# Linear attention with RMS norm and a Gelu feed-forward layer: two batches' keys without padding rows, Gelu's table loaded one step earlier

## The chip, the cores and the metric

The kernel runs on one core of one Trainium2 chip. The metric is the time of one execution on the device in microseconds (us). TensorE (PE in the profile) multiplies matrices, VectorE (DVE) and ScalarE (ACT) work element by element, GpSimd (POOL) helps them, and SyncE (SP) issues the transfers between the main memory and the core's own memory, which 16 DMA engines carry out.

## The reference

For each of 8 batches and 8 heads, keys and values of 576 rows are multiplied to a 64x64 matrix, the queries are multiplied by it, and the result is normed along the head. The heads side by side give 4608 rows of 512 numbers, which pass through a feed-forward layer with 2048 inner units and an exact Gelu. All is float32.

```python
# q, k, v: (8, 8, 576, 64); w_in: (512, 2048); w_out: (2048, 512)
kv = np.einsum('bhsd,bhse->bhde', k, v)
out = np.einsum('bhsd,bhde->bhse', q, kv)
rms = np.sqrt(np.mean(out * out, axis=-1, keepdims=True) + 1e-06)
x = (out / rms * g_norm).transpose(0, 2, 1, 3).reshape(8 * 576, 512)
h = x @ w_in
g = 0.5 * h * (1.0 + erf(h / np.sqrt(2)))
y = g @ w_out
```

## The kernel before

**Tiles and stages.** The 4608 rows are cut into seven chunks: two of 512 (`PLAIN`) and five of 704 or 736. A chunk's attention output is made while the chunk before goes through the feed-forward layer, so that TensorE always has matmuls. For the first chunk there is no chunk before: its keys, queries and weights have to arrive first, and this start-up is where the change lies.

**Keys and values.** They are summed over a batch's 576 rows in `sum_kv` (line 198), for one pair of heads at a time. The rows are split as 4 x 112 + 128. The 4 x 112 come as one tile, `kv_main[b, p]`, of 112 used partitions (`KROWS`) by 1024 numbers, which the host has padded with zeros to 128 partitions; the last 128 rows come as `kv_tail`. `load_kv(b, p)` issues both (line 161 for the main tile, lines 166 and 178 for the tail). Whatever the tile holds, TensorE reads its first 112 partitions only: line 162 cuts the view to `[:KROWS]`.

**The order of the transfers** is the order in which SyncE's instructions are written: batch 0's four key tiles with the first chunk's queries among them, the first weight, batch 1's first two pairs, the second weight (`w_in`), the first `w_out` and the next `w_in`, batch 1's other two pairs, then the remaining weights in turn. `load_w` (line 617) loads a weight. At most eight transfers are in flight: SyncE waits for the landing of the eighth before.

**The order of the work** on each engine is the order of the code; nothing is reordered. For the first chunk: `sum_first(p)` sums a pair's keys and `place_kv` copies the result (lines 209 on ScalarE, 211 on VectorE); `project_first` multiplies the queries (line 252). Then come the squares, their sums, and the reciprocal root (line 315 and three operations of VectorE). The first two blocks of the output are scaled on VectorE (lines 361, 864). For the other two, ScalarE spreads the roots (line 852), TensorE transposes them (line 872) and VectorE multiplies (line 874). Ahead of the transposes TensorE sums batch 1's first two pairs (line 198).

**The weights** arrive as 64-bit floats. `top_w(n)` (line 631) is a pass of ScalarE over a weight's upper halves, with Prelu; `bits_w(n)` (lines 641, 644) is VectorE's part, and gives the number in 32 bits. From that `high_w` (line 652, ScalarE) and `low_w` (line 656, VectorE) make a high and a low part. The output of the attention is split in the same way: `high_x` (line 369) makes four casts on ScalarE, `low_x` (line 374) four differences on VectorE.

**The feed-forward layer** of the first chunk: `layer1` multiplies by a block of the first weight (line 666 for the first two blocks, line 676 for the others), `gelu` applies Gelu twice on ScalarE (lines 689, 690), `rest` takes the low part on VectorE (line 696), `layer2` multiplies by the second weight (line 708). [...] The dummy Gelu at line 857, on two numbers, makes the compiler put the load of Gelu's table there (`ACT_TABLE_LOAD`) and not ahead of the first real Gelu.

Of the kernel before, what the change touches and what calls it, by code (L numbers as in the profile page):

```python
# [11 lines left out]
AF = mybir.ActivationFunctionType  # L12
# [4 lines left out]
P = 128  # L17
EPS = 1e-6
CH = 512
KROWS = 112  # L20
# [19 lines left out]
def linear_attn_rms_gelu_ffn(  # L40
# [18 lines left out]
    nc = tc.nc  # L59
# [66 lines left out]
    def block_tile(name, dtype):  # L126
        if name not in home:
            raise KeyError(name)
        width = 2 * WIDEST if name[0] == "d" else 2 * DM
        return home[name].tile([P, width], dtype, name=name)  # L130
# [3 lines left out]
    def late_tile(name):  # L134

        if name not in late:
            late[name] = block_tile(name, I32).bitcast(F32)
        return late[name]
# [11 lines left out]
    def load_kv(b, p):  # L150

        early = b == 0 or (b == 1 and p > 1)
        if early:
            main = late_tile(f"w_out{NF - 1 - p if b == 0 else NF - 3 - p}")
        elif b == PLAIN and p > 1:
            main = block_tile(f"x{2 + p}", F32)
        elif b == PLAIN + 1 and p > 1:
            main = block_tile(("w_in7", "w_out4")[p - 2], F32)
        else:
            main = low.tile([P, 2 * DM], I32, name="kv_main", bufs=2).bitcast(F32)  # L160
        nc.sync.dma_start(out=main, in_=kv_main[b, p])
        main = main.rearrange("p (a n) -> p a n", a=2)[:KROWS]
        if b == 0:
            tails = late_tile(f"w_in{NF - 1}")[:TAIL].rearrange("p (a n) -> p a n", a=NP)
            if p == 0:
                nc.sync.dma_start(out=tails, in_=kv_tail[0])
            tail = tails[:, p]
        else:
            if early:
                tail = late_tile(f"w_in{NF - 5}")[:, (p - 2) * 2 * P:(p - 1) * 2 * P]  # L170
            elif b >= PLAIN and p > 1:
                if p == 2:
                    kv_ps["tails"] = block_tile(SPARE[2], F32)
                tail = kv_ps["tails"][:, (p - 2) * 2 * P:(p - 1) * 2 * P]
            else:
                tail = low.tile([P, 2 * P], I32, name="kv_tail", bufs=2).bitcast(F32)
            tail = tail[:TAIL]
            nc.sync.dma_start(out=tail, in_=kv_tail[b, :, p])
        tail = tail.rearrange("p (a n) -> p a n", a=2)
        parts = [main[:, :, j * P:(j + 1) * P] for j in range(NJ)] + [tail]  # L180
        kv_in[b, p] = [(t[:, 0], t[:, 1]) for t in parts]
# [440 lines left out]
    def top_w(n):  # L622


        zs[n] = work.tile([P, WIDEST], I32, name="z", bufs=2)[:, :DM]
        top = raw[n].rearrange("p (n two) -> p n two", two=2)[:, :, 1]
        if n < FULL:
            z = late_tile(f"w_out{NF - 1}")[:, n * DM:(n + 1) * DM]
        else:
            z = work.tile([P, WIDEST], F32, name="w", bufs=2)[:, :DM]  # L630
        nc.scalar.activation(  # L631
            out=zs[n].bitcast(F32), in_=top.bitcast(F32), func=AF.Prelu,
            scale=2.0 ** -112, alpha=2.0 ** 32,
        )
        ws[n] = z.bitcast(I32)
# [91 lines left out]
    g_row = late_tile(f"w_in{NF - 6}")[:1, P:2 * P]  # L727
    ones, eps = (late_tile(f"w_in{NF - 6}")[:1, a * P:(a + 1) * P] for a in (2, 3))
    load_kv(0, 0)
    first.load(0)  # L730
    load_kv(0, 1)
    first.load(1)
    for p in (2, 3):
        load_kv(0, p)
# [32 lines left out]
    for d in range(0, 2 * D, BLK):  # L767
        h = d // D * D
        nc.gpsimd.tensor_tensor(
            out=fold[:, d:d + BLK], in0=ident[:, h:h + BLK], in1=ident[:, h + BLK:h + 2 * BLK],  # L770
# [24 lines left out]
    def column(n, t):  # L795
        return n_fold + 2 * ((n - 2) * NG + t)

    def sum_squares(n):
# [12 lines left out]
        out=half_g, in0=ps[:, :1], scalar1=0.5, scalar2=None, op0=ALU.mult  # L811
# [3 lines left out]
        out=sums[:, :P], lhsT=ones, rhs=eps, start=True, stop=False,  # L815
# [4 lines left out]
        out=root_g, in0=half_g, scalar1=D ** 0.5, scalar2=None, op0=ALU.mult  # L820
# [9 lines left out]
    for half in range(2):  # L830
# [6 lines left out]
        out=sums[:, :n_fold].rearrange("p (g b) -> p g b", g=2), lhsT=fold,  # L837
# [3 lines left out]
    for half in range(2):  # L841
        nc.scalar.activation(
            out=first.block((1, half)),
            in_=first.ps.pop((1, half)).rearrange("p (a n) -> p a n", a=2), func=AF.Copy,
# [4 lines left out]
    for n in (2, 3):  # L849
        roots[n] = low.tile([P, CH], F32, name="gh", bufs=2)  # L850
        at = column(n, 0)
        nc.scalar.copy(
            out=roots[n].rearrange("p (c d) -> p c d", d=D),
            in_=first.inv[:, at:at + 2 * NG].unsqueeze(2).broadcast_to((P, 2 * NG, D)),
        )
    top_w(1)
    nc.scalar.activation(out=eps[:, :2], in_=ones[:, :2], func=AF.Gelu)

    kv_ps[1, 0] = next_bank("a")
    sum_kv(1, (0, 1), kv_ps[1, 0])  # L860
    for half in range(2):
# [3 lines left out]
            out=first.o_all[:, half], in0=first.ps.pop((0, half)), scalar=root_g, in1=bc,  # L865
# [656 lines left out]
```

## Time and profile before

| what | value |
|---|---|
| median of 3 runs | 742.12 us (740.96 to 743.08) |
| the profiled execution | 741.02 us |
| its span, first to last instruction | 739.2 us |
| TensorE busy | 732.6 us (99%) |
| VectorE, ScalarE, GpSimd busy | 528.1, 357.3, 122.6 us |
| chain that ended last | TensorE 93%, transfers 3% |
| transfers | 233.66 MB, 316 GB/s on average |

The profile's page divides the span into 40 slices of 18.5 us. The chain that ended last is found by going back from the last instruction, at each step to whatever released it. An idle stretch is named with what ended it, in brackets behind an instruction. Of the 1.8 us between the profiled execution's time and its span the trace shows nothing.

### The profile page before, as it was taken

How to read it: one execution, taken by the hardware profiler on the slowest of the kernel's cores; microseconds unless marked ns; L12 is line 12 of the kernel's file. 1: busy time of each engine (PE TensorE's matmuls, PEld its weight loads, DVE VectorE, ACT ScalarE, POOL GpSimd, SP SyncE). 2: the span in 40 equal slices, each digit the busy share in tenths (PEclk: the TensorE clock that was granted, in tenths of full speed). 3: DMA queues.
4: the chain of work that ended last, by engine and by line, in shares of the span. 5: the costliest groups of instructions: out<-in, count | busy, mean ns of one | idle time of the engine just before them, and what ended most of it. 6: DMA issues, size and time to landing. Idle time of an engine off the chain costs nothing.

```text
span 739.2 us, 13288 instructions
## 1 busy us (share of the span) xinstructions
PE 732.6 (99%) x5150; PEld 696.3 (94%) x5150; DVE 528.1 (71%) x756; ACT 357.3 (48%) x565; POOL 122.6 (17%) x88
## 2 busy tenths in 40 slices
PE   8999999999999999999999999999999999999998
PEld 6888888888899999999999999999999999999997
DVE  3999998999857689357599257598257598254773
ACT  3788845643465367054365154365154364133640
POOL 1000000000045800013800014600015600022000
PEclk9999999999999999999999999999999999999999
DMA  9998985689998999988999978999978889988893
GB/s 343 407 408 284 364 283 200 220 313 359 346 335 314 361 336 387 408 317 282 323 325 371 406 243 271 313 326 361 395 230 281 276 291 310 335 295 289 295 318 121
DMA packets 84962, 233.66 MB, mean 316 GB/s; under 512 B 8484, under 2 KB 29476, under 8 KB 84900
## 3 DMA queue, kind: packets, MB, share of 16 engines
q1 hardware_dynamic: 84896, 232.82, 88.6%
q8 instruction: 41, 0.67, 0.4%
q14 instruction: 21, 0.17, 0.1%
q10 hardware_dynamic: 4, 0.00, 0.0%
HBM read 193.99 MB, written 38.80 MB: 315 GB/s over the span
## 4 chain that ended last, share of the span: by engine, by line
PE 93%; DMA 3%; DVE 1%; ACT 1%; issue 1%; ACTq 0%; DVEq 0%
PE banks_Z L1276 15%; PE banks_Z L1184 14%; PE acc L708 11%; PE h L676 10%; PE banks_X L1184 10%; PE banks_Y L1184 10%; PE banks_X L1276 10%; PE banks_Y L1276 9%; DMA w_out<-kv_main 1%; DMA w_in<-w_in 1%; PE banks_W L198 1%; PE banks_W L1184 1%; PE banks_W L414 1%; PE a L198 1%; PE banks_W L1276 0%
## 5 line engine op out<-in xcount | busy, mean ns | idle before, releaser
L1258 DVE TENSOR_TENSOR d<-d,d 128x704 fp32r<-128x704 f32 (+1 forms) x140 | 135.3, 988 | 33.8 <-ACT d L1254 33.6
L1254 ACT CAST d<-d 128x704 fp32r<-128x704 f32 (+1 forms) x140 | 105.0, 787 | 25.2 <-DVE d L1241 19.1
L604 DVE TENSOR_TENSOR e<-banks_Z,e 128x704 f32<-128x704 f32 (+1 forms) x53 | 47.7, 900 | 58.3 <-PE banks_Z L1184 46.8
L676 PE MATMUL h<-x,w_in 128*128 128x512 f32 x360 | 82.9, 380 | 0.0
L1276 PE MATMUL banks_X<-d,w_in 128*128 128x352 f32 (+1 forms) x504 | 79.1, 315 | 0.0
L1184 PE MATMUL banks_Z<-d,w_in 128*128 128x352 f32 (+1 forms) x468 | 78.0, 316 | 0.0
L676 PEld LDWEIGHTS h<-x,w_in 128*128 128x128 f32 x360 | 67.8, 189 | 10.1 <-ACT z L631 0.3
L708 PE MATMUL acc<-w_out,gh 128*128 128x512 f32 x256 | 77.0, 382 | 0.1
L1276 PEld LDWEIGHTS banks_X<-d,w_in 128*128 128x128 f32 x504 | 77.1, 189 | 0.0
L1184 PEld LDWEIGHTS banks_Z<-d,w_in 128*128 128x128 f32 x468 | 72.2, 189 | 1.1 <-DVE e L604 0.8
L1241 POOL TENSOR_TENSOR d<-d,d 128x704 f32<-128x704 f32 (+1 forms) x15 | 25.8, 1718 | 284.9 <-ACT d L1196 284.9
L1276 PE MATMUL banks_Y<-d,w_in 128*128 128x352 f32 (+1 forms) x432 | 67.2, 315 | 0.0
L1276 PEld LDWEIGHTS banks_Y<-d,w_in 128*128 128x128 f32 x432 | 66.1, 189 | 0.0
L1184 PE MATMUL banks_X<-d,w_in 128*128 128x352 f32 (+1 forms) x372 | 62.2, 317 | 0.0
L1184 PE MATMUL banks_Y<-d,w_in 128*128 128x352 f32 (+1 forms) x372 | 61.5, 315 | 0.0
L604 DVE TENSOR_TENSOR e<-banks_Y,e 128x704 f32<-128x704 f32 (+1 forms) x30 | 27.0, 903 | 47.4 <-PE banks_Y L1276 28.9
L1276 PE MATMUL banks_Z<-d,d 128*128 128x352 f32 (+1 forms) x360 | 59.8, 315 | 0.1
L1184 PEld LDWEIGHTS banks_X<-d,w_in 128*128 128x128 f32 x372 | 57.4, 189 | 1.4 <-issue 1.0
L1276 PE MATMUL banks_Z<-d,w_in 128*128 128x352 f32 (+1 forms) x360 | 57.9, 315 | 0.0
L1184 PEld LDWEIGHTS banks_Y<-d,w_in 128*128 128x128 f32 x372 | 57.6, 189 | 0.0
L1276 PEld LDWEIGHTS banks_Z<-d,d 128*128 128x128 f32 x360 | 55.8, 189 | 0.4 <-DVE d L1258 0.4
L708 PEld LDWEIGHTS acc<-w_out,gh 128*128 128x128 f32 x256 | 47.9, 189 | 8.5 <-issue 1.4
(228 smaller groups left out, 1129.7 us busy)
## 6 DMA issues: line engine op xcount, KB each, us to landing
w_in<-products_out SPq DMA_DIRECT2D x110, 512.0 KB, 4.8
w_in<-products_in SPq DMA_DIRECT2D x104, 512.0 KB, 4.8
d<-products_in SPq DMA_DIRECT2D x36, 512.0 KB, 5.1
d<-products_out SPq DMA_DIRECT2D x30, 512.0 KB, 4.6
products_in<-w_in SPq DMA_DIRECT2D x36, 256.0 KB, 5.2
w_in<-w_in SPq DMA_DIRECT2D x16, 512.0 KB, 10.2
w_out<-w_out SPq DMA_DIRECT2D x16, 512.0 KB, 10.2
products_out<-w_out SPq DMA_DIRECT2D x32, 256.0 KB, 5.3
```

The lines of the kernel that those rows point to most:

```text
L198: nc.tensor.matmul(out=ps[r, n * D:(n + 1) * D], lhsT=k[:, r], rhs=v[:, r], start=(j == 0), stop=(j == NJ),)
L414: nc.tensor.matmul(out=to[rows(h), :, at], lhsT=kv[b % 2][rows(half), p, h ^ half], rhs=q[rows(half), h, :, at], start=True, stop=True,)
L604: return eng.tensor_tensor(out=out, in0=x, in1=y, op=op)
L676: nc.tensor.matmul(out=h, lhsT=parts["in", i][:, w][:, p * P:(p + 1) * P], rhs=woven(at.x[p][:, x]), start=(m + p == 0), stop=(m == 2 and ...
L708: nc.tensor.matmul(out=ps, lhsT=x[:, ts], rhs=woven(parts["out", i][:, w]), start=(i == 0 and m == 0), stop=(m == 2 and i == NF - 1),)
L1184: nc.tensor.matmul(out=ps[:, n], lhsT=y, rhs=woven(x[:, z, kb]), start=k in (0, 2, 1) and kb + i == 0, stop=kb == 1 and i == 2, skip_group ...
L1241: eng.tensor_tensor(out=out, in0=x, in1=y, op=op)
L1254: nc.scalar.copy(out=t[:, 0], in_=self.source(k, n))
L1258: latest["low"] = nc.vector.tensor_tensor(out=t[:, 1], in0=src, in1=t[:, 0].bitcast(F32), op=ALU.subtract)
L1276: nc.tensor.matmul(out=self.last(k, a) if alone else ps[:, a], lhsT=y, rhs=woven(x[:, z, p]), start=(alone or k in (0, 2, 1)) and n + p + ...
```

## The change

Two edits. In `load_kv`, the main tiles of batches 0 and 1 are transferred with 112 partitions instead of 128; later batches are as before. The dummy Gelu moves from behind the second `top_w` to the place ahead of it, and the table load with it. The lines behind the first edit have numbers that are higher by one, up to the place of the second.

```diff
@@ load_kv
-        nc.sync.dma_start(out=main, in_=kv_main[b, p])
+        filled = KROWS if b < 2 else P
+        nc.sync.dma_start(out=main[:filled], in_=kv_main[b, p, :filled])
         main = main.rearrange("p (a n) -> p a n", a=2)[:KROWS]
@@ after the copies of the roots, ahead of batch 1's sums
+    nc.scalar.activation(out=eps[:, :2], in_=ones[:, :2], func=AF.Gelu)
     top_w(1)
-    nc.scalar.activation(out=eps[:, :2], in_=ones[:, :2], func=AF.Gelu)
```

SyncE's queue at the start of the program, up to the second weight. `w_out`, `w_in` and `kv_main` on the left of an arrow are buffers (the early tiles borrow room that weights use later), on its right the arrays in the main memory. Before:

```order
L161 DMA w_out_98<-kv_main 128x1024
L161 DMA w_out_100<-kv_main 128x1024
L225 DMA w_in_102<-qT 128x512 x2
L617 DMA w_in_107<-w_in 128x1024
L161 DMA kv_main<-kv_main 128x1024
L178 DMA kv_tail<-kv_tail 128x256
L161 DMA kv_main<-kv_main 128x1024
L178 DMA kv_tail<-kv_tail 128x256
L617 DMA w_in_117<-w_in 128x1024
```

Now:

```order
L162 DMA w_out_98<-kv_main 112x1024
L162 DMA w_out_100<-kv_main 112x1024
L226 DMA w_in_102<-qT 128x512 x2
L618 DMA w_in_107<-w_in 128x1024
L162 DMA kv_main<-kv_main 112x1024
L179 DMA kv_tail<-kv_tail 128x256
L162 DMA kv_main<-kv_main 112x1024
L179 DMA kv_tail<-kv_tail 128x256
L618 DMA w_in_117<-w_in 128x1024
```

The queue's order is the same; only the first dimension of the key tiles differs (eight of them, of which four are shown).

ScalarE, from the copies of the roots to the pass over the third `w_in`. `z` is what a pass writes, `x` the four casts. Before:

```order
L852 COPY gh<-y 128x512 x2
L631 ACTIVATE z<-w_in_117 128x512
L857 ACT_TABLE_LOAD
L857 ACTIVATE w_in_85<-w_in_85 1x2
L631 ACTIVATE z<-w_out_119 128x512
L369 CAST x_379<-o 128x512
L369 CAST x_381<-o 128x512
L369 CAST x_383<-o 128x512
L369 CAST x_385<-o 128x512
L631 ACTIVATE z<-w_in_121 128x512
```

Now:

```order
L853 COPY gh<-y 128x512 x2
L857 ACT_TABLE_LOAD
L857 ACTIVATE w_in_85<-w_in_85 1x2
L632 ACTIVATE z<-w_in_117 128x512
L632 ACTIVATE z<-w_out_119 128x512
L370 CAST x_379<-o 128x512
L370 CAST x_381<-o 128x512
L370 CAST x_383<-o 128x512
L370 CAST x_385<-o 128x512
L632 ACTIVATE z<-w_in_121 128x512
```

The load and the dummy Gelu have moved ahead of the pass over the second weight (`w_in_117`); all else stands as it stood.

## Rows read from the trace of the kernel before

**Rows 1.** The page: busy time of each engine, and the chain by engine.

```profile
PE 732.6 (99%) x5150; PEld 696.3 (94%) x5150; DVE 528.1 (71%) x756; ACT 357.3 (48%) x565; POOL 122.6 (17%) x88
...
PE 93%; DMA 3%; DVE 1%; ACT 1%; issue 1%; ACTq 0%; DVEq 0%
```

**Rows 2.** The chain in order of time, 0 to 45 us: start, length, what.

```profile
11.72 8.22 DMA w_in<-w_in
...
26.35 0.58 DVE gl L696
...
34.42 2.64 PE acc L708 x11
```

**Rows 3.** Busy time by stretch: PE, PEld, DVE, ACT, POOL, clock, DMA share, GB/s.

```profile
15.00:20.00 5.00, 4.14 (x64) 3.87 (x64) 3.43 (x8) 3.06 (x7) 0.00 (x0) 1.00 1.03 403
```

**Rows 4.** SyncE's queue in order of time: start of an issue, its length.

```profile
19.95 0.33 SPq L232 DMA_DIRECT2D q<-qT  x1
21.23 0.33 SPq L617 DMA_DIRECT2D w_in<-w_in  x1
22.52 0.33 SPq L617 DMA_DIRECT2D w_out<-w_out  x1
```

**Rows 5.** TensorE in order of time: start, length, line; idle time ahead in brackets.

```profile
11.84 0.69 PE L198 MATMUL a<-w_out 112*64 112x64 f32 x16 [0.21 <-DMA w_out<-kv_main]
...
16.68 0.69 PE L198 MATMUL a<-kv_main 112*64 112x64 f32 x16
...
18.34 0.69 PE L198 MATMUL a<-kv_main 112*64 112x64 f32 x16 [0.86 <-DMA kv_main<-kv_main]
...
19.07 1.10 PE L872 MATMUL acc<-w_in,gh 128*128 128x128 f32 x8
```

**Rows 6.** TensorE's weight loads in order of time, batch 0's third key tile.

```profile
10.82 0.55 PEld L198 LDWEIGHTS a<-w_out 112*64 112x64 f32 x16 [0.39 <-DMA w_out<-kv_main]
```

**Rows 7.** VectorE in order of time, 19 to 35 us.

```profile
19.77 0.69 DVE L874 TENSOR_TENSOR o<-o,acc 128x512 f32<-128x512 f32 x1 [0.45 <-PE acc L872]
...
21.12 0.75 DVE L864 SCALAR_TENSOR_TENSOR o<-acc,w_in,gl 128x512 f32<-128x512 f32 x1
...
22.38 0.42 DVE L641 TENSOR_SCALAR w_out<-z 128x512 int32<-128x512 int32 x1
...
24.50 1.28 DVE L374 TENSOR_TENSOR x<-o,x 128x512 fp32r<-128x512 f32 x2
26.35 0.69 DVE L696 TENSOR_TENSOR gl<-h,gh 128x512 fp32r<-128x512 f32 x1 [0.56 <-ACT h L690]
...
33.69 0.68 DVE L656 TENSOR_TENSOR w_out<-w,w_out 128x512 fp32r<-128x512 f32 x1
```

**Rows 8.** ScalarE in order of time, 17 to 27 us.

```profile
17.88 1.14 ACT L852 COPY gh<-y 128x512 f32<-128x512 f32 x2 [0.89 <-DVE y L317]
19.96 0.67 ACT L631 ACTIVATE z<-w_in 128x512 f32<-128x512 f32 x1 [0.94 <-DMA w_in<-w_in]
20.65 1.28 ACT L857 ACT_TABLE_LOAD   x1
21.94 0.20 ACT L857 ACTIVATE w_in<-w_in 1x2 f32<-1x2 f32 x1
22.05 0.66 ACT L631 ACTIVATE z<-w_out 128x512 f32<-128x512 f32 x1
22.62 2.16 ACT L369 CAST x<-o 128x512 fp32r<-128x512 f32 x4
...
25.75 0.57 ACT L690 ACTIVATE h<-h 128x512 f32<-128x512 f32 x1
```

**Rows 9.** TensorE's weight loads in order of time, around 34 us.

```profile
33.69 0.19 PEld L708 LDWEIGHTS acc<-w_out,gh 128*128 128x128 f32 x1
34.42 0.19 PEld L708 LDWEIGHTS acc<-w_out,gh 128*128 128x128 f32 x1 [0.55 <-DVE w_out L656]
```

**Rows 10.** DMA queues from 14 to 16 us: packets, MB, share of 16 engines.

```profile
q8 instruction: 1, 0.02, 3.5%
```

## Prediction

> **What bounds the kernel now.** The page first: TensorE is busy 99% of the span and holds 93% of the chain that ended last [rows 1]. So the end is moved only by what lies on the chain outside TensorE. The chain in order of time says where that is [rows 2]: up to 19.94 us it runs through transfers, the last of them the second weight's (issued 11.72, 8.22 long), then through ScalarE and VectorE, and at 34.42 it enters TensorE. The first stretch is the one place where the edits act, and what reaches the end is the move of that 34.42. Work behind it is nearly all TensorE, so I carry the move through to the end in full.
>
> Next, what limits each step before 34.42. The transfer engines are full: 403 GB/s at a busy share of 1.03 from 15 to 20 us [rows 3]. SyncE has eight transfers in flight and issues one when the eighth before it has landed, so its issue times are landing times: 19.95 (second weight), 21.23, 22.52 [rows 4], or 1.28 us for a tile of 512 KB. That tile is 128 rows of 4 KB; spread evenly over the 16 engines it is 8 rows for each, 0.16 us a row.
>
> TensorE meets the keys in its own order [rows 5]. It waits 0.21 us at 11.84 for batch 0's last tile and 0.86 us until 18.34 for batch 1's second; the weight load ahead of batch 0's third tile sits 0.39 us on a transfer [rows 6]. Behind the 0.86 stand the transposes of line 872 (19.07), and VectorE idles 0.45 us until 19.77 for them [rows 7]. From there VectorE has a single hole before 34.4: 0.56 us at 26.35, for line 690's Gelu, whose second half ScalarE ends at 26.32 [rows 7, 8]. TensorE waits once more, 0.55 us at 34.42, for VectorE's low part of a weight (33.69 plus 0.68) [rows 7, 9].
>
> **Part 1, the keys without padding.** Eight tiles lose 16 of 128 rows, no instruction is added or moved, and TensorE reads only the 112 anyway. If each engine now gets 7 rows, a tile takes 0.16 us less. Four tiles of batch 0 and two of batch 1 are ahead of the landing for which TensorE waits until 18.34: 6 x 0.16 = 0.96 us. Of this, 0.86 is the wait itself. The last 0.10 needs the work ahead to move too, and the transposes' own inputs with it (line 852's copies start at 17.88 [rows 8]): batch 0's third tile lands 0.48 earlier, which covers the 0.39, and its fourth 0.64 earlier, which covers the 0.21, so these come some 0.4 us earlier. The transposes, VectorE at 19.77 and the matmuls behind them then stand 0.96 us earlier, against a lower end of 0.86. The last two tiles, batch 1's third and fourth, are not waited for; they bring the weights behind them 1.28 us forward, so that no weight becomes the bound.
>
> No row of this trace shows a 112-row transfer, so this saving has two other ends. With a slowest engine still at 8 rows it is zero per tile. At the other end a tile may be slower: the nearest row is batch 1's second tile, whose data came at 18.34, while the one ahead of it was in use at 16.68 without a wait [rows 5]. There an instruction fetch of 1.1 us (3.5% of 16 engines in 2 us [rows 10]) sat on an engine, so that the queue lost about 1 us on one tile. I take -0.16, since rows per engine is what the 1.28 us measures, and keep 0 and +1.0 for the range.
>
> **Part 2, the table.** ScalarE's rows [rows 8]: copies to 19.02, 0.94 us idle for the second weight, its pass 19.96 to 20.63, table load 20.65 to 21.93, dummy Gelu from 21.94, and the next pass at 22.05. The load and the dummy thus take 1.40 us behind the weight's landing. After the edit they start at 19.02 and fill the idle time, and the pass starts at 20.42, 0.46 later than now. VectorE asks for this pass at 22.38 [rows 7], so it has 1.3 us to spare even when nothing else moves. The third pass can start when its weight has landed, 21.23 [rows 4], instead of 22.05; the four casts, which need VectorE's sum that ends at 21.87 (21.12 plus 0.75 [rows 7]), start at about 21.9 instead of 22.62. That is 0.7 us, and the chain behind (casts, a pass, two Gelus) ends at 25.6 rather than 26.32. VectorE is busy to 25.78, so its 0.56 us hole closes and VectorE sets the pace. What is late next is TensorE: its weight load was ready at 33.88 (33.69 plus 0.19 [rows 9]) and started at 34.42, so of the 0.56 it takes 0.54.
>
> Both together: VectorE starts 0.96 earlier; ScalarE's two Gelus end about 1.47 earlier (casts follow the pass of the third weight, now 20.45 to 21.1, and end at 23.2, Gelus at 24.85), VectorE is free for them at 25.78 - 0.96 = 24.82, so the hole keeps some 0.05. TensorE's 34.42 becomes 34.42 - 0.96 - 0.51 = 32.95; its own readiness, 33.88 - 0.96 = 32.92, agrees.
>
> **Sum.** The profiled execution took 741.02 us, 739.2 of it span. -0.96 and -0.51 give -1.5, so 739.5 on its terms. It is 1.1 us below the median of the runs, 742.12; on the median's terms the forecast is 740.6. Written with x, the change of one tile's time, the sum is -0.5 + 6x.
>
> [...]
>
> **Rivals.**
> 1. *The slowest share of a tile stays at 8 rows* (x = 0). [...] Against it: nothing in the rows says that a part is bound to fixed rows. Then part 2 alone remains: 742.12 - 0.5 = 741.6. If this last half microsecond is swallowed too, it is 742.1; that is in the same case.
> 2. *The 112-row transfers are slower than those with 128* (x above zero), the case on the other side. Mechanism: 7 rows each shift the shares against the partitions they wrote so far, two engines then write to the same place at the same time and one waits, and the queue of eight hands each delay on to all that follows. The place is TensorE's wait at 18.34, which has no slack, and six tiles stand ahead of it. Break-even is x = 0.5/6 = 0.08 us. From x = (2.2 + 0.5)/6 = 0.45 us, three rows' time lost per tile, it is slower by over 0.3%. At the upper end, x = 1.0, it is 742.12 - 0.5 + 6 = 747.6. For it: the queue is full, so any lost time is lost for good. Against it: each engine has fewer bytes to move, and no row here shows two engines holding each other up.
> 3. *The instruction fetch falls elsewhere*, within the forecast: when it comes after batch 1's second tile, up to 0.4 us more is gained before TensorE itself is the bound; when it hits another engine, as much may be lost.
>
> **How the numbers follow.** Forecast (x = -0.16) 0.45; rival 1 0.27; rival 2 0.28, about half of it below 0.45 us per tile. 0.3% of this kernel is 2.2 us, about what a measurement can tell from no change. Forecast and rival 1 lie inside that, so most of their chance is "same"; runs of the kernel spread by 0.15% either way, which lets the forecast reach beyond 0.3% one time in five (0.09), rival 1 rarely (0.02). Faster 0.11, slower 0.17 (the larger half of rival 2 and a little noise), same 0.72. The range starts 1.2 us below the forecast (noise and rival 3), at 739.4, and goes up to 744.8, half-way into rival 2 (x about 0.5): nearly all of the forecast and of rival 1, and half of rival 2, some 8 in 10.
>
> **What would show it.** In the profile of the changed kernel: TensorE's wait for batch 1's second tile gone and its transposes near 18.1 instead of 19.07 (part 1); the second weight landing near 19.0 instead of 19.94; ScalarE's table load right behind line 853's copies, casts 1.4 us earlier, VectorE's hole ahead of the first Gelu remainder under 0.1 us (part 2); the chain entering TensorE for good near 33.0. With rival 1 the second weight lands at 19.9 as now and only the hole is gone; with rival 2 it lands after 20.5, and TensorE waits longer than 0.86 us for the same tile. A gap of TensorE behind 35 us that was not there before would make the carrying-through wrong.

## The result and the profile after

The changed kernel took 746.39 us (median of 6 runs, 744.34 to 747.09); the kernel before 741.65 us (median of 6, among them the three known ahead of the prediction). The ratio is 1.0064, with a 95% interval of 1.0051 to 1.0077: 4.7 us slower. The runs of the kernel before that were made beside the experiments have medians of 740.95 us (15 runs) and 740.66 us (22 runs). The prediction said 740.6 us and gave a range up to 744.8, so both its sign and its range were wrong. The profiled execution of the changed kernel took 747.09 us, 745.3 of it span.

The page first. TensorE is still busy 99% of the span, and 4.8 us longer than in [rows 1], although it has the same 5150 instructions. The row of its granted clock shows why: the second slice of 18.6 us has a 7 and the first an 8.

```profile
PE 737.4 (99%) x5150; PEld 701.3 (94%) x5150; DVE 528.1 (71%) x756; ACT 357.8 (48%) x565; POOL 122.5 (16%) x88
...
PEclk8799999999999999999999999999999999999999
...
PE 96%; DMA 2%; issue 1%; DVE 1%; ACT 0%; ACTq 0%
```

Busy time by stretch, with the columns of [rows 3]. Two things are new. The transfer engines are as busy as before (share 1.03 to 1.05), yet from 5 to 20 us they move 281 to 293 GB/s, where they moved 368 to 403 before, and 261 instead of 411 from 25 to 30 us. And the granted clock is 0.50 from 15 to 25 us, where it was 1.00 before.

```profile
5.00:10.00 5.00, 4.35 (x55) 3.45 (x55) 0.76 (x4) 0.21 (x1) 0.00 (x0) 1.00 1.04 293
10.00:15.00 5.00, 3.14 (x56) 2.31 (x53) 0.89 (x4) 1.51 (x4) 0.00 (x0) 0.87 1.03 281
15.00:20.00 5.00, 4.30 (x35) 3.11 (x31) 2.57 (x6) 2.73 (x6) 0.00 (x0) 0.50 1.05 282
20.00:25.00 5.00, 5.00 (x54) 4.76 (x54) 2.38 (x6) 2.09 (x5) 0.00 (x0) 0.50 1.03 365
25.00:30.00 5.00, 5.00 (x22) 4.51 (x21) 4.24 (x8) 4.35 (x9) 0.00 (x0) 0.77 1.04 261
```

SyncE's queue, whose issue times are landing times as in [rows 4]: an issue comes when the eighth transfer before it has landed. The landing of the second weight, which released the issue at 19.95 in [rows 4], now releases it at 23.06. The landing of the fourth `w_in` tile, a block of the feed-forward layer's first weight, shows at 35.31.

```profile
23.06 0.33 SPq L233 DMA_DIRECT2D q<-qT  x1
...
35.31 0.33 SPq L618 DMA_DIRECT2D w_out<-w_out  x1
```

In the kernel before, that last row stands at 29.71:

```profile
29.71 0.33 SPq L617 DMA_DIRECT2D w_out<-w_out  x1
```

So six tiles delay the second weight by 3.1 us (0.52 each) and eight delay the fourth `w_in` by 5.6 us (0.70 each).

TensorE in order of time, with the columns of [rows 5]. It now waits for three of batch 0's four key tiles, 2.2 us in all, where [rows 5] had 0.21 for the last one. Behind them its sum of batch 1's second key tile takes 1.07 us instead of 0.69, at a granted clock of 0.50, and the transposes of line 873 start at 24.50, where [rows 5] had 19.07.

```profile
9.55 0.69 PE L199 MATMUL a<-w_out 112*64 112x64 f32 x16 [0.65 <-DMA w_out<-kv_main]
...
12.33 0.69 PE L199 MATMUL a<-w_out 112*64 112x64 f32 x16 [0.53 <-DMA w_out<-kv_main]
...
14.17 1.12 PE L199 MATMUL a<-w_out 112*64 112x64 f32 x16 [1.03 <-DMA w_out<-kv_main]
...
23.29 1.07 PE L199 MATMUL a<-kv_main 112*64 112x64 f32 x16
...
24.50 1.97 PE L873 MATMUL acc<-w_in,gh 128*128 128x128 f32 x8
```

The chain in order of time, as in [rows 2]: transfers of keys to 14.03, then almost only TensorE, from 15 to 25 us at the clock of 0.50. Line 253's products (matrix multiplications of TensorE) start at 43.14; in the chain of before (the second fence) the same products, there line 252, start at 37.06.

```profile
5.32 8.71 DMA w_out<-kv_main
...
43.14 1.03 PE a L253 x17
```

```profile
37.06 1.03 PE a L252 x17
```

The move of this point, 6.08 us, is the whole difference of the two spans (745.3 - 739.2 = 6.1). In this execution all the loss is made in the first 43 us, and nothing is lost or won behind it.

The early table load did its part. ScalarE loads the table right behind its copies, and VectorE's first Gelu remainder (line 697), which had waited 0.56 us in [rows 7], starts without idle time, but five microseconds later.

```profile
24.52 1.28 ACT L857 ACT_TABLE_LOAD   x1
```

```profile
31.59 0.68 DVE L697 TENSOR_TENSOR gl<-h,gh 128x512 fp32r<-128x512 f32 x1
```

### The profile page after: what moved, and what is told of

Its sections match the earlier page's. It is cut to its first block, busy times and chain, and to the rows that moved or that the text cites. A ratio compares the mean times of both kernels' runs of the same rounds, so it can differ in the third digit from the quotient of the medians.

```text
span 745.3 us, 13288 instructions
## 1 busy us (share of the span) xinstructions
PE 737.4 (99%) x5150; PEld 701.3 (94%) x5150; DVE 528.1 (71%) x756; ACT 357.8 (48%) x565; POOL 122.5 (16%) x88
## 4 chain that ended last, share of the span: by engine, by line
PE 96%; DMA 2%; issue 1%; DVE 1%; ACT 0%; ACTq 0%
PE banks_Z L1277 14%; PE banks_Z L1185 14%; PE acc L709 11%; PE h L677 11%; PE banks_X L1185 10%; PE banks_Y L1185 10%; PE banks_X L1277 10%; PE banks_Y L1277 9%; DMA w_out<-kv_main 2%; PE a L199 1%; PE banks_W L199 1%; PE h L667 1%; PE banks_W L1185 1%; PE banks_W L415 1%; PE h L803 1%
## 5 line engine op out<-in xcount | busy, mean ns | idle before, releaser
L1185 PEld LDWEIGHTS banks_Z<-d,w_in 128*128 128x128 f32 x468 | 72.2, 189 | 1.1 <-DVE e L605 0.8
L1277 PEld LDWEIGHTS banks_Z<-d,w_in 128*128 128x128 f32 x360 | 55.4, 189 | 0.0
```

Source lines behind the costliest of these rows:

```text
L1185: nc.tensor.matmul(out=ps[:, n], lhsT=y, rhs=woven(x[:, z, kb]), start=k in (0, 2, 1) and kb + i == 0, stop=kb == 1 and i == 2, skip_group ...
L1277: nc.tensor.matmul(out=self.last(k, a) if alone else ps[:, a], lhsT=y, rhs=woven(x[:, z, p]), start=(alone or k in (0, 2, 1)) and n + p + ...
```

## The experiments

Two causes stand in this profile: transfers without the padding take longer (by 0.52 to 0.70 us a tile), and TensorE's granted clock falls to 0.50 around its waits for them. Either could make the five microseconds. The first runs split the change into its parts and measured the transfers by themselves; the next ones took the clock's fall away, then took one batch's tiles at a time.

**Each part alone.** The table only, on the kernel before:

```
+    nc.scalar.activation(out=eps[:, :2], in_=ones[:, :2], func=AF.Gelu)
     top_w(1)
-    nc.scalar.activation(out=eps[:, :2], in_=ones[:, :2], func=AF.Gelu)
```

> Only the table load moves; the keys are transferred with 128 rows as before. Working of the prediction: VectorE's hole of 0.56 us ahead of the first Gelu remainder closes and TensorE's 34.42 becomes 33.9, so 0.5 us less than before, 0.999 of it. Rival (the half microsecond is lost behind): no difference. Either way the 112-row transfers are then the whole cause of the loss.

The rows only, on the kernel before:

```
+        filled = KROWS if b < 2 else P
-        nc.sync.dma_start(out=main, in_=kv_main[b, p])
+        nc.sync.dma_start(out=main[:filled], in_=kv_main[b, p, :filled])
```

> Only the keys' 112 rows; the table load stands where it was. If the rows are the whole cause: slower than the changed kernel by what the table brings, 0 to 0.5 us, so 4.7 to 5.3 us above before (1.0065 to 1.007). Rival (the early table load helps to make the loss): clearly less than 4.7 us above before.

Measured: the table alone 740.36 us, 0.9994 [0.9985, 1.0003] of before; the rows alone 746.53 us, 1.0079 [1.0065, 1.0093]. So the rows alone make the loss (5.6 us between the medians), and no part of it is the table's. The table's own gain is not shown: the ratio stands for some 0.4 us, but its interval includes 1. ScalarE's rows with the table alone stand close to where the prediction put them: load at 19.02, the second weight's pass at 20.43 (20.42 was said), casts at 21.55 (21.9 was said).

```profile
19.02 1.28 ACT L856 ACT_TABLE_LOAD   x1
...
20.43 0.65 ACT L631 ACTIVATE z<-w_in 128x512 f32<-128x512 f32 x1
...
21.55 2.16 ACT L369 CAST x<-o 128x512 fp32r<-128x512 f32 x4
```

```profile
25.27 0.69 DVE L696 TENSOR_TENSOR gl<-h,gh 128x512 fp32r<-128x512 f32 x1
```

VectorE's row of the Gelu remainder behind them has no idle time ahead of it, so the hole of 0.56 us is closed. Of the 0.8 us by which this execution's span is shorter (738.4 against 739.2) not all is the table's, though: batch 1's second key tile came about half a microsecond earlier than in [rows 5], 17.81 against 18.34, with no change to its transfer.

```profile
17.81 0.69 PE L198 MATMUL a<-kv_main 112*64 112x64 f32 x16 [0.35 <-DMA kv_main<-kv_main]
```

**The transfers by themselves.** A kernel of nothing but transfers of one tile of 4 KB rows, 24 of a kind behind each other, eight in flight as in the kernel. The stretch with 112 rows differs from the one with 128 like this:

```
     for n in range(24):
-        nc.sync.dma_start(out=t[n], in_=src(n))
+        nc.sync.dma_start(out=t[n][:112], in_=src(n)[:112])
```

There are others with 96, 64 and 32 rows, with 112 and 128 rows by turns, in two halves of 64 rows, and in two halves of the columns.

> A kernel that only transfers: stretches of 24 tiles from the main memory, rows of 4 KB, in nine shapes one after the other; the rest of the computation is left out and the outputs are zeros. Theory A (the place written decides: with other than 128 rows two engines write to the same part of the memory at a time, and one waits): 112 rows take 1.5 to 2.0 us a tile (448 KB at the 281 GB/s that the changed kernel showed from 10 to 15 us are 1.6 us), 64 rows nearly as long as 128 (1.1 to 1.3 us), 32 rows about 0.6, 128 rows cut into two halves of 64 rows 2.2 to 2.6 us, cut into two halves of columns 1.28 as in one piece, all at a busy share near 1.0. Rival B (only the rows per engine count): 112, 96, 64, 32 rows take 1.12, 0.96, 0.64, 0.32 us, and both ways of halving 1.28. Rival C (a 112-row transfer goes to fewer engines): busy share clearly under 1.0 in its stretch.

Stretches in the middle of each kind; the columns are the stretch, VectorE, GpSimd, the granted clock, the busy share of the transfer engines, and GB/s. In this order: 112 rows, 96, 64, 32, 112 and 128 by turns, halves of rows, halves of columns, 128 rows.

```profile
62.00:86.00 24.00, 0.00 (x0) 0.00 (x0) 1.00 1.03 247
100.00:124.00 24.00, 0.00 (x0) 0.00 (x0) 1.00 1.03 262
138.00:158.00 20.00, 0.00 (x0) 0.00 (x0) 1.00 1.04 204
166.00:179.00 13.00, 0.00 (x0) 0.00 (x0) 1.00 1.04 203
192.00:212.00 20.00, 0.00 (x0) 0.00 (x0) 1.00 1.03 275
232.00:264.00 32.00, 0.00 (x0) 0.00 (x0) 1.00 1.03 262
280.00:300.00 20.00, 0.00 (x0) 0.00 (x0) 1.00 1.06 387
312.00:328.00 16.00, 0.00 (x0) 0.00 (x0) 1.00 1.03 410
```

A tile of 128 rows (524,288 bytes) takes 1.28 us at 410 GB/s; one of 112 rows (458,752 bytes) takes 1.86 us at 247. Leaving out an eighth of the bytes makes the tile 45% longer: x is +0.58 us, not -0.16. By turns with 128 rows, a pair takes 3.57 us instead of 2.56: 1.0 us more, where 0.58 was to be expected from the 112 rows alone. Even 64 rows take as long as 128 (1.28 us). In all these stretches the busy share is 1.03 to 1.06, so rival C (fewer engines) falls; each packet lasts longer. Worked out from the share, the rate and 16 engines (1.03 x 16 x 4096 bytes at 410 GB/s), a packet of 4 KB takes 0.16 us on average with 128 rows, and likewise 0.27 with 112 and 0.33 with 64. So it is not that a few engines had more rows while the others stood idle.

Whether the number of rows or their place decides, a second kernel of the same kind told: 64 rows at partitions 0 to 63, at 32 to 95 and at 64 to 127; 112 rows at 16 to 127 and at 0 to 111.

```
-        nc.sync.dma_start(out=t[n][:64], in_=src(n)[:64])
+        nc.sync.dma_start(out=t[n][32:96], in_=src(n)[32:96])
```

> A kernel that only transfers, as the first of this kind: stretches of 24 tiles with rows of 4 KB, 128 rows, then 64 rows written to partitions 0 to 63, to 32 to 95, to 64 to 127, then 112 rows to partitions 16 to 127 and to 0 to 111, and 128 rows again; the computation is left out and the outputs are zeros. The three stretches of 64 rows have the same shape and bytes and differ in the place alone. Theory P (the place decides: some partitions share one way into the memory, and two engines meet there): the 64 rows from 32 on take clearly less than the 1.30 us that those from 0 on took, down to half of it. Rival N (the number of rows decides, through the way in which the rows are shared out): 1.30 us for all three. 112 rows 1.87 us at either place.

Time from issue to landing, with eight in flight, of the 64 rows at 0 to 63, at 32 to 95 and at 64 to 127, then of the 112 rows at 16 to 127 and at 0 to 111, and of 128 rows:

```profile
DMA to landing us min/median/max: 9.7/10.1/12.3
```

```profile
DMA to landing us min/median/max: 4.8/4.9/9.6
```

```profile
DMA to landing us min/median/max: 7.1/10.0/10.4
```

```profile
DMA to landing us min/median/max: 10.7/14.7/14.9
```

```profile
DMA to landing us min/median/max: 15.0/15.2/15.4
```

```profile
DMA to landing us min/median/max: 10.1/10.2/14.4
```

With eight in flight, an eighth of the median is an estimate of a tile's time: 1.26 us, 0.61, 1.25, then 1.84, 1.90 and 1.28. For 32 to 95 it is on the low side, for the transfer engines were not full there (a share of 0.96); by the rate of 372 GB/s in the stretch below it is 0.70 us.

```profile
92.00:102.00 10.00, 0.00 (x0) 0.00 (x0) 1.00 0.96 372
```

As many rows with as many bytes thus take about half the time when they lie across the middle, and a packet of 4 KB, worked out as above, takes 0.17 us there, about as with 128 rows, instead of the 0.33 of 0 to 63. So the place decides, and the number of bytes does not. The edit moves the rows in the main memory along with those in the core's own; that it is the latter that counts was not tested by itself. For it speaks that a tile cut into halves of rows, which reads the same rows in the same order as a whole one, takes 2.00 us a pair, and one cut into halves of columns 1.35.

112 rows take 1.90 us at 0 to 111 and 1.84 at 16 to 127; why both are slower than 128 rows is not shown. That two engines write to the same place at the same time, as rival 2 put it, would fit the longer packets (0.27 us against 0.16), but no run showed which engine wrote which row.

**Without the clock's fall.** The changed kernel with ten products that nobody reads, put where TensorE waits. The first line below stands in `sum_first`, ahead of batch 0's second, third and fourth tiles, the second ahead of `sum_squares(2)`, the others at batch 1's first two tiles:

```
+        keep_warm((0, 1, 1, 2)[p])
...
+    keep_warm(2)
...
-    sum_kv(1, (0, 1), kv_ps[1, 0])
+    keep_warm(2)
+    sum_kv(1, (0,), kv_ps[1, 0])
+    keep_warm(2)
+    sum_kv(1, (1,), kv_ps[1, 0])
```

> The changed kernel with ten extra dummy matmuls in TensorE's waits at the start (1, 1 and 2 ahead of batch 0's second, third and fourth sums, 2 ahead of the sums of squares, 2 each ahead of batch 1's two sums). [...] Rival (the clock is only a companion, the late landings set everything): 746.4 or more, as the changed kernel.

Measured: 746.1 us, 1.0071 [1.0057, 1.0084]; no gain on the change's 1.0064. It is nearer to the rival's 746.4 than to 744.3, the author's estimate for a fall of the clock that costs some 2 us of its own. The clock did stay up, at 1.00, here from 15 to 20 us:

```profile
15.00:20.00 5.00, 4.32 (x45) 3.71 (x44) 2.76 (x6) 3.01 (x6) 0.00 (x0) 1.00 1.05 294
```

The chain now runs through the landings: the fourth `w_in` lands at 34.95, then come a ScalarE pass and VectorE's parts of the weight, and the chain enters TensorE at 38.47.

```profile
25.26 9.69 DMA w_in<-w_in
...
38.47 2.64 PE acc L709 x11
41.11 1.03 PE a L253 x17
```

Line 253's products start at 41.11, 2.03 us earlier than in the changed kernel, but 4.05 later than before. So the fall of the clock lies over a delay that the landings alone would make. Of the 2.03 us, the span kept 0.9 (744.4 against 745.3): from 145 to 222 us TensorE's weight loads wait once, for 1.0 us, for a key tile, which they do neither before nor in the changed kernel. Its waits there (in all, times, longest):

```profile
PEld a L199 <- DMA w_out<-kv_main: 1.0, 1, 1.0
```

Why that tile comes late was not followed up; the timed runs show no gain at all.

This chain gives a rule that the prediction had not worked out: the chain can enter TensorE 3.5 us after the fourth `w_in` has landed (38.47 - 34.95). Before, that landing was at 29.7 and would have asked for an entry at 33.2; the entry was at 34.42 [rows 2]. This weight thus had 1.2 us of slack, and 34.95 - 29.7 - 1.2 makes 4.05 us, the delay that is seen. In the changed kernel the landing at 35.31 asks for an entry at 38.8, and so for line 253's products, 2.64 us behind the entry, at 41.5; they came at 43.14. By this estimate some 4.4 us of the 6.1 are the landings' and some 1.7 the clock's.

**One batch at a time.** Both kernels have the early table; the one leaves out the padding of batch 0's four tiles only, the other of batch 1's:

```
-        filled = KROWS if b < 2 else P
+        filled = KROWS if b == 0 else P
```

```
-        filled = KROWS if b < 2 else P
+        filled = KROWS if b == 1 else P
```

Two theories stood against each other. By theory L the late landings alone set the loss. By theory C the waits for batch 0 bring the granted clock down, as to the 0.50 of the changed kernel, and that carries the rest: 4 to 5 us with batch 0's tiles alone, 1 us at most with batch 1's.

> The changed kernel with 112 rows for batch 0 only (four tiles). The landings of batch 0 are as late as in the changed kernel (fourth tile 2.3 us late), those behind stay about 2.5 us late and grow no more. Theory L (late landings alone set the loss): about half of the changed kernel's loss, 1.5 to 2.5 us above before. [...]

> The changed kernel with 112 rows for batch 1 only (four tiles). Nothing is late up to 14 us, the clock stays at 1.00; batch 1's second tile comes 1.0 to 1.3 us later than before, and the fourth w_in, which landed at 29.7 us, near 32. Theory L: 1 to 2 us above before. [...]

Batch 1 alone: 743.09 us, 1.0031 [1.0019, 1.0043]; batch 0 alone: 743.16 us, 1.0046 [1.0031, 1.0061]. Batch 1's median is 2.4 us above before, more than the 1 to 2 us of theory L and the 1 us of theory C; its profile is of the fastest of five executions (741.69 us, 1.0 above), and of the other four, at 742.88 to 744.37, two have a mean granted clock of 0.994 and 0.995. With batch 1's tiles alone TensorE waits 1.37 us instead of 0.86 for the second of them, and the chain again goes through the fourth `w_in`:

```profile
18.90 0.69 PE L199 MATMUL a<-kv_main 112*64 112x64 f32 x16 [1.37 <-DMA kv_main<-kv_main]
```

```profile
21.70 9.92 DMA w_in<-w_in
...
35.09 2.64 PE acc L709 x11
```

The landing is 1.9 us later than before, and the entry 3.5 us behind it, at 35.09: by the rule 1.9 - 1.2 = 0.7 us of delay, and 0.67 is seen (35.09 - 34.42).

Batch 0's runs fall into two groups: 742.11, 742.19, 742.95, 743.01 and 743.3 us at a mean granted clock of 0.994 to 1.000, and 745.79, 745.91 and 746.49 at 0.991. The first stands 1.5 to 2.6 us above before, as theory L had it, the second 5.1 to 5.8, even more than theory C had. The first group's profile (742.11 us) shows a clock of 1.00 throughout, as from 15 to 20 us here:

```profile
15.00:20.00 5.00, 4.44 (x70) 3.72 (x65) 3.62 (x9) 3.31 (x7) 0.00 (x0) 1.00 1.04 398
```

To see the other group, the same kernel was run twice more:

> The kernel with batch 0's 112 rows only, once more for its profile: its eight times fell into two groups, 742.1 to 743.3 and 745.8 to 746.5 us, and the profile taken was of the first, with a clock of 1.00 throughout. Theory C2 (the waits of batch 0 bring the clock down in some executions and not in others, and that alone makes the second group): a time near 746 comes with a clock near 0.5 between 14 and 26 us and landings as before; a time near 742.5 with 1.00. Rival: a time near 746 at a clock of 1.00.

> The same kernel a third time, with the same two theories: a time near 746 with a clock near 0.5 between 14 and 26 us (theory C2), or at a clock of 1.00 (rival).

They took 746.5 and 748.04 us, and in both the clock fell: it stands at 0.50 from 15 to 25 us. The first of them from 15 to 20 us:

```profile
15.00:20.00 5.00, 4.30 (x38) 3.11 (x32) 2.51 (x6) 2.67 (x6) 0.00 (x0) 0.50 1.05 404
```

The landings differ much less than the times: the second weight's shows at 21.59 in the 742.11 us execution and at 22.35 and 22.30 in the other two. The chains of the execution of 742.11 us (the first fence) and of that of 746.5 us leave the keys' transfers 0.9 us apart (13.51 and 14.41) and come to line 253's products 4.5 us apart, with the same work of TensorE between:

```profile
4.98 8.53 DMA w_out<-kv_main
...
37.94 1.03 PE a L253 x17
```

```profile
5.41 9.00 DMA w_out<-kv_main
...
42.42 1.03 PE a L253 x17
```

So from 742.11 to 746.5 us, 4.4 us, the landings can make 0.8 to 0.9. Here, where four tiles are late and not eight, the fall of the clock is itself the larger cost, the other 3.5 us or so. The kernel before has it too in some executions: at a mean granted clock of 0.999 or more it took 740.3 to 741.5 us, at 0.993 743.88, at 0.995 742.49 and 742.88. What starts the fall isn't settled. The three waits for batch 0's keys were 0.73, 0.41 and 0.99 us in the execution that kept its clock, 1.06, 0.81 and 0.94 in the one that lost it (746.5 us), but 0.65, 0.53 and 1.03 in the changed kernel, which lost it too.

The same ten dummy products, all in the same places, on this kernel (the other lines as above):

```
-        filled = KROWS if b < 2 else P
+        filled = KROWS if b == 0 else P
...
+        keep_warm((0, 1, 1, 2)[p])
...
```

> As the kernel with batch 0's 112 rows only, with ten extra dummy matmuls in TensorE's early waits. [...] Theory L: no difference to the kernel without the dummies beyond noise.

Measured: 743.67 us, 1.0045 [1.0031, 1.0059]. That is 3.0 us above before, where theory C gave 1.5 to 2.5. The profile keeps a clock of 1.00, but the chain waits for batch 1's second key tile until 20.34, and the time is no lower than without the products.

```profile
9.95 10.39 DMA kv_main<-kv_main
```

Without them, in the execution of 742.11 us, TensorE summed that tile at 19.12 without a wait. Between the two lies SyncE's longest gap between two issues from 10 to 25 us: with the products it stands at 14.59 to 17.40, ahead of this tile's landing, without them at 19.37 to 21.59, behind it. So the products do more than hold the clock, and this run tells nothing against either cause. The fetch of 16 KB of instructions of [rows 10], 1.1 us on one transfer engine, is one thing that moves: in the kernel before it begins between 14 and 16 us, in the changed kernel between 18 and 20 (3.9% of 16 engines in these 2 us). That it makes the gap is not shown.

**Leaving out the padding with full tiles.** If 128 rows are what a transfer wants, the padding can be left out by another layout: batch 0's keys of a pair as 4 x 128 rows, and the tails of 64 rows, two pairs one above the other, in one tile of 128 rows for all pairs (the table early too):

```
+        if b == 0:
+            nc.sync.dma_start(out=main, in_=full_main[p])
...
+            tails = late_tile(f"w_in{NF - 1}")[:, :4 * P]
+            if p == 0:
+                nc.sync.dma_start(out=tails, in_=full_tail)
+            tail = tails[p % 2 * D:(p % 2 + 1) * D, p // 2 * 2 * P:(p // 2 + 1) * 2 * P]
```

> The early table load, all transfers with 128 rows, and the padding of batch 0 taken away in another way: its 576 rows are split as 4 x 128 + 64 and the last 64 rows of two pairs share one tile of 128 partitions, so that the four pairs' tails are 256 KB instead of 512 KB. If bytes count as long as all 128 rows are written: 256 KB at 0.64 us earlier landings from batch 0's second tile on, hence 0.64 us less besides the 0.4 of the early table load, about 1.0 us less than before (0.9986). Rival (the start no longer hangs on landings when the table is early): 0.4 us less, as with the table alone.

Measured: 740.99 us, 1.0006 [0.9992, 1.0019]; the gain of 1 us isn't there. Five of its twelve executions have a mean granted clock of 0.998 or less and took 741.63 to 745.39 us; but the other seven, with a median of 740.51, are no more than 0.1 us under those of the kernel before that kept their clock (740.58). The transfers have their old rate again (403 GB/s from 10 to 15 us), and the second weight's landing shows at 19.47, which is no earlier than in the kernel with the table alone (19.42). TensorE waits 0.86 us for the second key tile, and the clock of this execution fell to 0.66 in one stretch. Why that tile isn't earlier stays open.

```profile
8.81 0.69 PE L211 MATMUL a<-w_out 128*64 128x64 f32 x16 [0.86 <-DMA w_out<-full_main]
```

```profile
10.00:15.00 5.00, 4.93 (x62) 3.71 (x64) 1.43 (x7) 1.53 (x5) 0.00 (x0) 0.66 1.03 403
```

No version here is shown to be faster than the kernel before; the table alone is the only one whose ratio lies below 1.

## Why the prediction was wrong

- **The step that failed is the sign and the size of x.** "I take -0.16, since rows per engine is what the 1.28 us measures." All transfers behind that 1.28 us had 128 rows, so the row could not tell rows per engine from rows per place in the memory. The transfers alone gave +0.58 us; the kernel 0.52 to 0.70. The forecast's six tiles were to bring 0.96 us; instead the landing behind them came 3.1 us later.
- **Rival 2 had the mechanism that the runs bear out** (transfers of 112 rows take longer, 1.86 us against 1.28, and the queue hands the delay on), and its sign that the second weight would land after 20.5: it landed at 23.06. It had a chance of 0.28, and the range was cut inside it at about x = 0.5. With the 0.58 that was measured its sum gives 742.12 - 0.5 + 3.5 = 745.1 us, still 1.3 short. Its full upper end, 747.6, would have held the time, but by luck: x = 1.0 with six tiles stands there for 0.6 to 0.7 with eight and a fallen clock. That two engines meet at one place, its reason, fits the packets and is not shown.
- **Its deciding place was wrong.** It put the price at TensorE's wait at 18.34, with six tiles ahead. Without the clock's fall the fourth `w_in` decides: eight tiles are ahead of it, and it had 1.2 us of slack. The prediction used these two last tiles only with a negative x ("no weight becomes the bound") and did not ask the same for a positive one. With the kernel's own 0.70 per tile, 8 x 0.70 - 1.2 = 4.4 us of the 6.1 that the profiled execution lost; the formula of the prediction, -0.5 + 6 x 0.58, gives 3.0.
- **The fall of the clock was in no rival.** Before, the granted clock was 1.00 from 15 to 20 us [rows 3], and the prediction did not ask what longer waits would do to it. In the changed kernel it lies over the landings' delay (1.7 to 2.03 us at line 253's products in the profiles, no gain in the timed runs when it was held up); with batch 0's tiles alone it costs some 3.5 us where it happens. How much of the changed kernel's 4.7 us is the clock's stays open.
- **Rival 1**, x = 0, fell with the forecast. No run shows its term, a slowest share that stays at 8 rows; the tile of 112 rows took 1.86 us, that of 128 rows 1.28. **The fetch of instructions** (rival 3) did move, from between 14 and 16 us to between 18 and 20; what that is worth no run tells apart.
- **Part 2's mechanism was right, its size is not shown.** The pass at 20.43 and the closed hole stand as predicted; casts at 21.55 owe part of their lead to a key tile that landed earlier. -0.5 us was said, and the measured ratio of 0.9994 has an interval that includes 1. In the changed kernel, where the landings and the clock decide, no gain of part 2 can be seen (746.39 us with it, 746.53 with the rows alone).
- **Carrying the move through to the end was right in the profile of the changed kernel:** 6.08 us at line 253's products, 6.1 at the span. It carried a loss instead of a gain. With the dummy products 1.1 us more was lost behind.

## What to carry to other kernels

On a full transfer queue, price a transfer of another shape by a measurement of that shape, not by its bytes: here 112 rows took 45% longer than 128 (1.86 us against 1.28), so padding that fills the 128 partitions was cheaper to move than to leave out. When a delay may go either way, follow it with both signs to every landing that has slack, and compare the slack with the number of transfers ahead of it. Where an early wait of TensorE grows, ask also what its clock will do; in the changed kernel it was 0.50 for some 10 us behind such waits.

## What the runs showed of the hardware

- A tile of 4 KB rows takes 1.28 us with 128 rows, 1.86 with 112, 1.50 with 96, 1.28 with 64 (at 0 to 63), 0.61 to 0.70 with 64 at 32 to 95, and 0.65 with 32, always with eight in flight and, for all but the fifth (0.96), the transfer engines at a busy share of 1.03 or more. A full share thus says nothing of the rate: it stood beside 203 and beside 410 GB/s.
- Cutting a tile into two halves by rows takes 2.00 us for the pair; by columns, 1.35.
- Transfers of 112 and 128 rows by turns take 3.57 us a pair, where 1.86 and 1.28 would make 3.14; which of the two loses the rest is not shown.
- In the changed kernel the granted clock was 0.50 from 15 to 25 us, and 0.87 on average in the five us ahead; TensorE waited three times, for 0.5 to 1.0 us, between 8.9 and 14.2 us. With batch 0's tiles alone the clock fell in some executions and not in others, with waits that differ by 0.5 us at most.
